# PV of four head groups per run in a fused attention and gated FFN block

## The chip, the cores and the metric

The kernel runs on one core of one Trainium2 chip. Its time is device microseconds of one execution, median of several. TensorE (PE in the profile) does the matmuls, PEld is its weight loads, VectorE is DVE, ScalarE is ACT, GpSimd is POOL, and SyncE (SP) issues most of the DMA transfers.

## The reference

One sequence of 2048 tokens of width 576 in bf16. A layer norm, then attention with 32 heads of 18 elements in a sliding window of 256 tokens, then a gated FFN of width 4608 on the same normalised input, and the two are multiplied:

```python
def _A_ref(x, wqkv, wo):
    H = 32; Dh = D // H; W = 256
    q, k, v = ...                       # (x @ wqkv) in heads
    scores = jnp.einsum("bhqd,bhkd->bhqk", q, k) * (Dh ** -0.5)
    mask = (i - j >= 0) & (i - j < W)
    p = _softmax(jnp.where(mask, scores, -1e9), axis=-1)
    o = jnp.einsum("bhqk,bhkd->bhqd", p, v)
    return o.reshape(B, S, D) @ wo

def _B_ref(x, w_gate, w_up, w_down):
    h = _sigmoid(x @ w_gate) * (x @ w_up)
    return h @ w_down

xn = _layernorm(A_x)
s = _A_ref(xn, A_wqkv, A_wo)
g = _silu(_B_ref(xn, B_w_gate, B_w_up, B_w_down))
return A_x + s * g
```

## The kernel before

The tokens are worked in four chunks of 512. For each chunk the kernel makes a graph of operations (layer norm, V, Q and K, attention of eight groups of four heads, output projection, FFN), and a list scheduler in the kernel's own Python puts the operations of all chunks into one fixed order for each engine. The engines then run their lists and wait on semaphores. FFN matmuls fill the places where attention would make TensorE wait.

Nearly all matmuls are pairs: two matmuls of 64 rows that run side by side in the two row halves of the array. All of them come from one helper, so they stand under one line (L122) in the profile:

```python
def pair(eng, outs, lhs, rhs, start, stop, swap=0):
    for i in range(2):
        t = i ^ swap
        res = eng.matmul(outs[i], lhs(ROWS[t], i), rhs(ROWS[t], i), start=start, stop=stop, tile_position=(64 * t, 0))
```

Attention of one head group computes the scores transposed, keys on the partitions, exponentiates them with ScalarE into a ring of bf16 tiles (`expr`, NEX = 12 slots), and masks the diagonal blocks with VectorE. When two head groups are ready, one PV run multiplies V by the weights. It works in tiles of 64 rows and 32 columns, eight at a time, and V carries a column of ones, so that the sum of the softmax comes out as a nineteenth row:

```python
def build_pv(self, c, pr):
    pend, self.pend = self.pend, []          # two head groups
    hp = self.pool_s.hold()                  # one PSUM unit of two banks
    def f_pv(eng):
        outs = self.halves(hp, NT)
        for n, ks in enumerate(kss):         # 12 blocks of 64 keys (8 in the first chunk)
            q0, q1 = span[ks]
            cols = slice(q0 * SW, q1 * SW)   # 64 to 320 queries
            for g, (hg, where, _) in enumerate(pend):
                for t in range(2):
                    for i in range(2):
                        res = eng.matmul(outs[i][p0:p0 + VH, cols], self.v_aug[ROWS[i], o:o + VH],
                                         self.expr[ROWS[i], se, t, cols], ...,
                                         tile_position=(64 * i, p0))
    pv = op("PE", est, f_pv, ...)            # one operation: nothing stands between its matmuls
    for i in range(2):                       # VectorE: transpose, 1/sum, multiply, transpose
        t1 = ...; hp.release(t1); rc = ...; on = ...; t2 = ...
        # then DMA of each head's rows to oT
```

The PSUM has four units: `pool_s = Pool("S", [0, 1])` for attention and `pool_f = Pool("F", [2, 3, 1])` for the FFN. The attention weights stay in SBUF for the whole run, loaded once:

```python
wq, wk, wv = (self.wqkv[:, i * D:(i + 1) * D] for i in range(3))
self.op_wqk = [self.load_nat(self.wqk[:, :, i, :], w, "dma:wqk", ...) for i, w in enumerate((wq, wk))]
self.op_wv = [self.load_nat(self.wv_sb[:, :, :], wv, "dma:wv", ...)]
self.op_wqk4 = [op("DVE", ..., copy of wqk's last 64 columns to wq4), four smaller copies]
...
self.op_wo_w = [self.load_nat(self.wo_sb[:, :, :], self.wo, "dma:wo", ...)]   # after the second head group
```

From the second chunk on, x is loaded to `xr` (two slots) and normalised into `xnr`, which a DMA transposes to `xnT`.

Of the kernel before, what the change touches and what calls it, by code (L numbers as in the profile page):

```python
# [8 lines left out]
D = 576  # L9
H = 32  # L10
DH = 18
F = 4608
P = 128
KB = 5
RD = 64
XW = D + RD
NHG = H // 4
NFT = F // P
NT = 512
# [10 lines left out]
SW = 64  # L30
# [6 lines left out]
NEX = 12  # L37
OENG = ("SP", "POOL")
PV_ORDER = (0, 5, -4, -3, -2, -1, 1, 2, 3, 4, 6, 7)
TURN_NS = 265.0  # L40
# [13 lines left out]
NXR = 2  # L54
NXN = 2
NST = 3
NQD = 2
NFIN = 2
NTH = 4
NTAIL = 112  # L60
# [13 lines left out]
NQK = 5  # L74

# [10 lines left out]
SPACE_NS = ((1500, 1500, 1400, 1500, 2000, 1200, 2000, 1100),  # L86
            (900, 1600, 1500, 1500, 1500, 2500, 1500, 1600),
            (1700, 900, 1500, 1500, 1500, 1500, 2000, 1500),
            (1500, 1500, 2500, 1100, 1600, 1500, 900, 1100))
# [4 lines left out]
def mm_ns(n):  # L94
    return max(24.7, n / 2.4 + 2.7)
# [38 lines left out]
def dve_ns(n, rate=1.0):  # L134
    return n / (0.96 * rate) + 160.0


class Hold:

    __slots__ = ("pool", "n", "units", "rel")  # L140

    def __init__(self, pool, n):
        self.pool = pool
        self.n = n
        self.units = None
        self.rel = []

    def release(self, op):
        self.rel.append(op)


class Pool:
# [27 lines left out]
    def take(self, hold, units):  # L180
        deps = []
        for u in units:
            if self.last[u] is not None:
                deps += self.last[u].rel
            self.last[u] = hold
        hold.units = units
        return deps


class Op:  # L190
# [3 lines left out]
    def __init__(self, eng, est, fn, name, deps, prio, nbytes, odeps, acq):  # L194
        self.eng = eng
        self.est = float(est)
        self.fn = fn
        self.name = name
        self.deps = []
        seen = set()  # L200
        stack = list(deps)
        while stack:
            d = stack.pop(0)
            if d is None:
                continue
            if isinstance(d, (list, tuple)):
                stack = list(d) + stack
            elif id(d) not in seen:
                seen.add(id(d))
                self.deps.append(d)  # L210
        self.prio = prio
        self.start = None
        self.end = None
        self.tok = None
        self.needs_tok = False
        self.nbytes = nbytes
        self.idx = -1
        self.succs = []
        self.cidx = -1
        self.odeps = [d for d in odeps if d is not None]  # L220
        self.acq = acq
        self.lane = None
        self.slack = 0.0
        self.filler = None
        self.space = 0.0
        for d in self.odeps:
            assert d.eng == eng

# [21 lines left out]
class Builder:  # L250
# [38 lines left out]
    def alloc_memory(self):  # L289
# [30 lines left out]
        self.ot1, _ = seq("ot1", [P, 1, NT], f32)  # L320
        self.o2, _ = seq("o2", [P, 1, NT])
        self.o2T, _ = seq("o2T", [P, 2, NT])
        self.oT, _ = seq("oT", [P, KB, NT])
        self.s_attn, _ = seq("s_attn", [P, BPC, D])
        self.wqk, _ = seq("wqk", [P, KB - 1, 2, D])
        self.wqkr, _ = seq("wqkr", [P, D])
        self.wq4, _ = seq("wq4", [P, KB, 2, RD])
        self.wv_sb, _ = seq("wv_sb", [P, KB - 1, D])
        self.wvr, _ = seq("wvr", [P, D // 2])
        self.wo_sb, _ = seq("wo_sb", [P, KB - 1, D])  # L330
        self.wor, _ = seq("wor", [P, D // 2])
        self.qd, _ = seq("qd", [P, NQD, 2, NT])
        self.xr, _ = seq("xr", [P, NXR, D])
# [23 lines left out]
    def build_graph(self):  # L357
        self.r_xr = Ring(NXR, "xr")
# [4 lines left out]
        self.r_kx = Ring(NKX, "kx")  # L363
        self.r_ex = Ring(NEX, "expr")
        self.r_ot1 = Ring(1, "ot1")
        self.r_o2 = Ring(1, "o2")
        self.r_o2T = Ring(2, "o2T")
# [19 lines left out]
        self.x_dma = {}  # L387
        self.op_wgr = {}
# [22 lines left out]
    def load_x(self, c, i=0):  # L411
# [8 lines left out]
        for _ in range(2):  # L420
            s_, d_ = self.r_xr.produce()
            slots.append(s_)
            dd += d_
        assert slots[1] == slots[0] + 1
        o = self.dma(self.xr[:, slots[0]:slots[0] + 2, :],
# [3 lines left out]
        for j in range(2):  # L429
            self.x_dma[st + j] = (o, self.xr[:, slots[j], :])  # L430
# [9 lines left out]
    def build_consts(self):  # L440
# [16 lines left out]

        wq, wk, wv = (self.wqkv[:, i * D:(i + 1) * D] for i in range(3))
        self.op_wqk = [self.load_nat(self.wqk[:, :, i, :], w, "dma:wqk", ("wqk", i), 5) for i, w in enumerate((wq, wk))]
        self.op_wqk += self.load_rem(self.wqkr[:, :], (wq, wk), "dma:wqkr", ("wqkr",), 5)  # L460
        for o in self.op_wqk:
            o.slack = 2500.0
        self.op_wv = [self.load_nat(self.wv_sb[:, :, :], wv, "dma:wv", ("wv",), 6)]
        self.op_wv += self.load_rem(self.wvr[:, :], (wv[:, 0:288], wv[:, 288:D]), "dma:wvr", ("wvr",), 6)
        for o in self.op_wv:
            o.slack = 5000.0
        self.op_wqk4 = [op("DVE", 420, lambda e: e.tensor_copy(self.wq4[:, 1:KB, :, :], self.wqk[:, :, :, 512:D]), "init:wq4",
                           deps=self.op_wqk, prio=2)]
        for t in range(2):
            for i in range(2):  # L470
                self.op_wqk4.append(op("DVE", 130, lambda e, t=t, i=i: e.tensor_copy(
                    self.wq4[ROWS[t], 0, i, :], self.wqkr[ROWS[1 - i], 512:D]), f"init:wq4:{t}{i}", deps=self.op_wqk, prio=2))
# [36 lines left out]
    def build_ln(self, c):  # L509
# [3 lines left out]
        for i in range(BPC):  # L513
# [24 lines left out]
            sn, dn = self.r_xn.produce()  # L538
# [17 lines left out]
            if c:  # L556
                self.r_xr.release(i % 2, ap)
# [56 lines left out]

    def build_qk(self, c, gi):
        op = self.op
        xs = par = c % 2
# [4 lines left out]
        gc = slice(gi * P, (gi + 1) * P)  # L622

        def lhs(r, t, k):
            if gi == 4:
                return self.wq4[r, k, :, :].rearrange("p i c -> p (i c)")
            return self.wqk[r, k - 1, t, gc] if k else self.wqkr[r, gc]
# [4 lines left out]
        pj = self.two("qk", f"{c}:{gi}", n, h, lhs, rhs, [self.op_xnT[c], self.op_wqk if gi < 4 else self.op_wqk4, dq], n)  # L632
# [44 lines left out]
    def build_v(self, c):  # L677
        op = self.op
        xs = c % 2
        for i in range(BPC):  # L680
# [5 lines left out]
            vp = self.row_proj("v", st, h, lambda r, k, cols=cols: self.xnT[r, xs, k, cols], self.wv_sb, self.wvr,  # L686
                               [self.op_xnT[c][i], self.op_wv, war])
# [16 lines left out]
    def build_attn(self, c, hg):  # L704
# [21 lines left out]
        for vi, (specs, groups) in enumerate(zip(bins, masks)):  # L726
# [27 lines left out]
            for g0, ng, m0, m1 in groups:  # L754
# [10 lines left out]
                mk = op("DVE", dve_ns(2 * ng * (m1 - m0) * SW, 2.0), f_mk, f"mk:{c}:{hg}:{vi}:{g0}", deps=[ex, self.op_mask], prio=1)  # L765
# [6 lines left out]
        if hg % 2:  # L772
            self.build_pv(c, hg // 2)
        if (c, hg) == (0, 1):
            pv = self.op_pv[(c, hg)]
            self.op_wo_w = [self.load_nat(self.wo_sb[:, :, :], self.wo, "dma:wo", ("wo",), 8, [pv])]
            self.op_wo_w += self.load_rem(self.wor[:, :], (self.wo[:, 0:288], self.wo[:, 288:D]), "dma:wor", ("wor",), 8, [pv])

    def build_pv(self, c, pr):
        op = self.op  # L780
        pend, self.pend = self.pend, []
        hp = self.pool_s.hold()
# [5 lines left out]
        def f_pv(eng):  # L788
            res = None
            outs = self.halves(hp, NT)  # L790
            for n, ks in enumerate(kss):
                q0, q1 = span[ks]
                cols = slice(q0 * SW, q1 * SW)
                for g, (hg, where, _) in enumerate(pend):
# [10 lines left out]
        est = TURN_NS + sum(mm_ns((b - a) * SW) for a, b in span.values())  # L805
# [5 lines left out]
        for i in range(2):  # L811
# [6 lines left out]
            def f_t1(e, i=i, p1=p1):  # L818
                return e.transpose(self.ot1[:, p1, :], self.halves(hp, NT)[i])  # L819
            t1 = op("DVE", dve_ns(NT), f_t1, f"ot:{c}:{pr}:{i}", deps=[pv, d1], prio=1)  # L820
            hp.release(t1)
            rc = op("DVE", 255, lambda e, o1=o1: e.reciprocal(o1[:, :, DH], o1[:, :, DH]), f"rc:{c}:{pr}:{i}", deps=[t1], prio=1)
            on = op("DVE", dve_ns(NT // 32 * DH), lambda e, o1=o1, o2=o2: e.tensor_tensor(
                o2[:, :, 0:DH], o1[:, :, 0:DH], o1[:, :, DH:VH].broadcast_to([P, NT // 32, DH]), ALU.mult),
                f"on:{c}:{pr}:{i}", deps=[rc, d2, self.op_o2z], prio=1)
            self.r_ot1.release(p1, on)
            t2 = op("DVE", dve_ns(NT), lambda e, p2=p2, p3=p3: e.transpose(self.o2T[:, p3, :], self.o2[:, p2, :]),  # L827
                    f"ot2:{c}:{pr}:{i}", deps=[on, d3], prio=1)
# [8 lines left out]
        if pr == 0:  # L837
            self.op_o[c].append(op("DVE", dve_ns(NT, 4.0), lambda e: e.tensor_copy(self.oT[ROWS[1], 0, :], self.oT[ROWS[0], 0, :]), f"odup:{c}",
                                   deps=[self.op_o[c], self.wo_last], prio=1))
# [15 lines left out]
    def build_wo(self, c):  # L855
        op = self.op
        last = []
        for i in range(BPC):
# [7 lines left out]
            wo = self.row_proj("wo", qb, h2, lambda r, k, cols=cols: self.oT[r, k, cols], self.wo_sb, self.wor,  # L866
                               [self.op_o[c], self.op_wo_w, war])
# [315 lines left out]

    def emit(self):
# [20 lines left out]

        outs = [i for lane, i in self.lane_ids.items() if lane[0] == "out"]
# [4 lines left out]
        def run_engine(e, eng):  # L1211
            known = {}
            for o in self.prog[e]:
# [4 lines left out]
                waits = {}  # L1218
                for d in o.deps:
                    k, v = d.tok  # L1220
                    if waits.get(k, -1) < v:
                        waits[k] = v
                for k, v in waits.items():
                    if known.get(k, -1) >= v:
                        continue
                    known[k] = v
                    eng.wait_ge(semof(k), v)  # L1227
# [52 lines left out]
```

The softmax here doesn't subtract the row's maximum and nothing guards it: scores larger than these inputs give would overflow.

## Time and profile before

| | |
|---|---|
| time, median of 3 | 559.3 us (558.81 to 559.37) |
| span of the profiled execution | 557.7 us |
| busy: PE, PEld, DVE, ACT, POOL | 552.4, 339.1, 333.6, 274.3, 210.3 us |
| granted TensorE clock | 1.00 throughout |
| moved by DMA | 67.83 MB, mean 122 GB/s |

The page gives each engine's busy time, the span in 40 slices, the DMA queues, the chain of work that ended last, and groups of instructions by line. L122 is the helper of the paired matmuls, L801 the matmul of PV, L819 the first transpose after PV, L764 the mask, L949 the multiplication that ends an FFN tile. A matmul's record is longer than its share of the array, since matmuls are pipelined: a 512-column pair shows 0.376 us, but the next pair starts 0.216 us after it. So costs on TensorE are read from the starts.

### The profile page before, as it was taken

The page shows a single profiled execution, that of the slowest core. Times are in us where ns is not written, and L with a number is a line of the kernel's source. Part 1 is how long each engine was busy: PE and PEld are TensorE (multiplying, and loading weights), DVE is VectorE, ACT ScalarE, POOL GpSimd, SP SyncE. Part 2 cuts the span into 40 slices and gives each one's busy share as a digit, 9 for nine tenths or more (in the row PEclk, how much of TensorE's full clock was granted, in tenths as well). Part 3 has the DMA queues.
Part 4 walks back from the last instruction along what each step waited for, and adds up shares of the span by engine and source line. Part 5 has one row for each costly group of instructions (what it writes and reads, how often), then busy time and mean ns, then how long its engine had stood idle before and what let it go on. Part 6 is the DMA issues. An engine that isn't in the chain of part 4 may idle for free.

```text
span 557.7 us, 19262 instructions
## 1 busy us (share of the span) xinstructions
PE 552.4 (99%) x8342; PEld 339.1 (61%) x8342; DVE 333.6 (60%) x797; ACT 274.3 (49%) x383; POOL 210.3 (38%) x360
## 2 busy tenths in 40 slices
PE   8999999999999999999999999999999999999997
PEld 7454444677755545457886555645588754444787
DVE  5477788787568667674558757357567623333133
ACT  4245654443656655645656464565756433223011
POOL 5564456566245454440667434034382200000000
PEclk9999999999999999999999999999999999999999
DMA  7988997831125535534121264234511035552010
GB/s 217 323 234 190 223 264 211 213 58 45 53 73 155 159 108 145 142 108 96 29 63 44 72 192 123 82 117 140 171 31 38 24 115 148 169 151 68 2 45 24
DMA packets 113468, 67.83 MB, mean 122 GB/s; under 512 B 18620, under 2 KB 111516, under 8 KB 113384
## 3 DMA queue, kind: packets, MB, share of 16 engines
q1 hardware_dynamic: 105960, 60.68, 39.7%
q0 software_dynamic: 7424, 5.92, 4.0%
q8 instruction: 66, 1.08, 0.8%
q14 instruction: 18, 0.15, 0.1%
HBM read 55.15 MB, written 2.36 MB: 103 GB/s over the span
## 4 chain that ended last, share of the span: by engine, by line
PE 98%; DVE 1%; DMA 0%; issue 0%; DVEq 0%
PE ps L122 95%; PE ps L801 3%; DMA x<-in_A_x_dram 0%; DVE small L525 0%; DVE small L527 0%; DVE xnr L541 0%; PE ps L599 0%; DVE s_attn L1062 0%; DVE thf L1067 0%; DVE xnr L545 0%; DVE small L529 0%; DVE small L531 0%; DVE xf L1072 0%; DVEq L1227 0%
## 5 line engine op out<-in xcount | busy, mean ns | idle before, releaser
L122 PE MATMUL ps<-xnT,wgs 64*128 64x512 bf16 (+1 forms) x2400 | 282.6, 368 | 0.2
L751 ACT ACTIVATE expr<-ps 128x1024 bf16<-128x1024 f32 (+4 forms) x160 | 154.9, 969 | 77.8 <-PE ps L122 77.2
L122 PEld LDWEIGHTS ps<-xnT,wgs 64*128 64x128 bf16 x2400 | 113.9, 94 | 115.0 <-DVE hT L949 1.6
L122 PE MATMUL ps<-wd_sb,hT 64*128 64x288 bf16 (+2 forms) x2448 | 156.7, 276 | 0.0
L949 DVE SCALAR_TENSOR_TENSOR hT<-tring,ps 128x512 bf16<-128x512 bf16 x144 | 98.3, 683 | 94.7 <-ACT tring L946 93.6
L946 ACT ACTIVATE tring<-ps 128x512 bf16<-128x512 f32 x144 | 86.1, 598 | 129.6 <-PE ps L122 127.5
L122 PEld LDWEIGHTS ps<-wd_sb,hT 64*128 64x128 bf16 x2448 | 112.5, 94 | 28.5
L279 POOL DMA_DIRECT2D qk<-qd x160 | 82.2, 521 | 119.9 <-PE ps L122 109.6
L764 DVE TENSOR_TENSOR expr<-expr,mask 128x128 bf16<-128x128 bf16 (+2 forms) x240 | 63.6, 299 | 62.3 <-ACT expr L751 61.7
L715 POOL TENSOR_SCALAR kx<-kprev,small 128x256 bf16<-128x256 bf16 x64 | 61.3, 967 | 28.2 <-PE ps L122 27.4
L122 PE MATMUL ps<-qk,kx 64*128 64x320 bf16 (+1 forms) x704 | 59.4, 254 | 0.0
L279 POOL DMA_DIRECT2D oT<-o2T x72 | 36.4, 513 | 58.7 <-DVE o2T L827 49.8
L122 PE MATMUL ps<-xnT,wgr 64*128 64x512 bf16 (+1 forms) x300 | 56.0, 367 | 0.0
L122 PEld LDWEIGHTS ps<-qk,kx 64*128 64x128 bf16 x704 | 31.2, 94 | 21.5 <-ACT expr L751 0.6
L122 PE MATMUL ps<-xnT,wqk 64*128 64x512 bf16 x256 | 32.6, 376 | 0.0
L1052 ACT ACTIVATE thf<-ps 128x576 bf16<-128x576 f32 (+3 forms) x22 | 11.4, 519 | 39.7 <-PE ps L122 39.4
L819 DVE STREAM_TRANSPOSE ot<-ps 128x512 f32<-128x512 f32 x32 | 22.4, 700 | 11.6 <-PE ps L801 11.5
L715 DVE TENSOR_SCALAR kx<-qk,small 128x512 bf16<-128x512 bf16 x64 | 22.4, 378 | 4.7 <-PE ps L122 4.1
L122 PEld LDWEIGHTS ps<-xnT,wgr 64*128 64x128 bf16 x300 | 14.9, 94 | 16.5
L827 DVE STREAM_TRANSPOSE o2T<-o 128x512 bf16<-128x512 bf16 x32 | 22.7, 711 | 1.0
L637 DVE CAST qd<-ps 128x1024 bf16<-128x1024 f32 (+1 forms) x20 | 22.1, 1111 | 1.5 <-PE ps L122 1.5
L697 ACT ACTIVATE v_aug<-ps 64x288 bf16<-64x288 f32 x32 | 13.1, 409 | 17.3 <-PE ps L122 16.8
(71 smaller groups left out, 300.9 us busy)
## 6 DMA issues: line engine op xcount, KB each, us to landing
wgs<-in_B_w_gate_dram SPq DMA_DIRECT2D x72, 256.0 KB, 3.3
wgs<-in_B_w_up_dram SPq DMA_DIRECT2D x72, 256.0 KB, 3.9
wd_sb<-in_B_w_down_dram SPq DMA_DIRECT2D x9, 576.0 KB, 6.3
qk<-qd POOLq DMA_DIRECT2D x100, 36.0 KB, 2.6
wgr<-in_B_w_gate_dram SPq DMA_DIRECT2D x36, 64.0 KB, 2.3
wgr<-in_B_w_up_dram SPq DMA_DIRECT2D x36, 64.0 KB, 2.7
xf<-in_A_x_dram SPq DMA_DIRECT2D x16, 144.0 KB, 2.6
out_dram<-xf SPq DMA_DIRECT2D x15, 144.0 KB, 1.8
```

Of the source, the lines that this page charges most:

```text
L122: res = eng.matmul(outs[i], lhs(ROWS[t], i), rhs(ROWS[t], i), start=start, stop=stop, tile_position=(64 * t, 0))
L279: o = self.op(eng, DMA_ISSUE_NS[eng], lambda e: e.dma_start(dst, src), name, deps, prio, nbytes=nbytes)
L637: return eng.tensor_copy(dst, self.both(h, n))
L697: return eng.activation(dst, src, ACTF.Copy)
L715: return e.tensor_scalar(self.kx[:, sx, pos:pos + n_ // SW, t, :], src.rearrange("p (s k) -> p s k", k=SW), self.half[:, t:t + 1], None, A ...
L751: return eng.activation(self.expr[:, se, :, lo * SW:NT], self.both(h, NT)[:, :, lo * SW:NT], ACTF.Exp, scale=SM_SCALE)
L764: return eng.tensor_tensor(e_, e_, m_, ALU.mult)
L801: res = eng.matmul(outs[i][p0:p0 + VH, cols], self.v_aug[ROWS[i], o:o + VH], self.expr[ROWS[i], se, t, cols], start=n == 0, stop=n == len( ...
L819: return e.transpose(self.ot1[:, p1, :], self.halves(hp, NT)[i])
L827: t2 = op("DVE", dve_ns(NT), lambda e, p2=p2, p3=p3: e.transpose(self.o2T[:, p3, :], self.o2[:, p2, :]), f"ot2:{c}:{pr}:{i}", deps=[on, d3 ...
L946: th = op("ACT", act_ns(NT), lambda e: e.activation(self.tring[:, st, :], bank(h, 0), ACTF.Tanh, scale=0.5), f"th:{c}:{ft}", deps=[pg, dt_ ...
L949: mu = op("DVE", dve_ns(NT), lambda e: e.scalar_tensor_tensor(self.hT[:, ft, :], self.tring[:, st, :], 1.0, bank(h, 1), ALU.add, ALU.mult) ...
```

## The change

PV waits for four head groups in place of two (PVG = 2 pairs), and one operation does both pairs one after the other, into two PSUM units that are given back one by one. There are eight PV runs in place of sixteen. That is meant to halve the changes between the tile shapes of PV and of everything else. Four groups need 20 slots of `expr` in place of 12. The SBUF for these comes from the attention weights: wq and wk are loaded anew in each chunk, 128 columns at a time, into a ring of two; wv and wo share one buffer and are loaded anew in each chunk, each when the other's last matmul is done; `wq4` and its copies fall away, since the last 64 columns are loaded straight into place; `xr` falls away, x being loaded into `xnr` and normalised in place; `qd` has one slot. Idle instructions (`nop`) on TensorE, spread over the FFN operations ahead of a run, are to place the run's first instruction at 80 to 124 of a block of 256 instructions. The wanted spacing of the score operations (SPACE_NS, a table for the scheduler) is set anew.

```diff
-NEX = 12
+NEX = 20
+NWQ = 2
+PVG = 2
-NXR = 2
-NQD = 2
+NQD = 1
+EVAC = (1, 0)
+HALF = 256
+PHASE = 73
+PV_PHASE = (80, 124)
+WAITS_FREE = 2
@@ SPACE_NS: all 32 values anew (cut)
@@ class Hold
+    def split(self):
+        self.parts = [Hold(self.pool, 1) for _ in range(self.n)]
@@ load_x
-        o = self.dma(self.xr[:, slots[0]:slots[0] + 2, :],
+        o = self.dma(self.xnr[:, slots[0]:slots[0] + 2, RD:XW],
@@ weights
-        self.op_wqk = [...]; self.op_wv = [...]; self.op_wqk4 = [...]; self.op_wo_w = [...]
+    def load_proj(self, c, w, name):
+        _, d = self.r_wvo.produce()
+        o = [self.load_nat(self.wvo[:, :, :], w, f"dma:{name}:{c}", ("wvo",), 6, d)]
+        o += self.load_rem(self.wvor[:, :], (w[:, 0:288], w[:, 288:D]), ...)
+    def load_qk(self, c, gi):
+        sw, d = self.r_wq.produce()
+        n = P if gi < 4 else RD
+        cols = [self.wqkv[:, i * D + gi * P:i * D + gi * P + n] for i in range(2)]
+        for i, w in enumerate(cols):
+            o.append(self.load_nat(dst, w, f"dma:wqk:{c}:{gi}", ("wqk", sw, i), 5, d))
@@ build_attn
-        if hg % 2:
-            self.build_pv(c, hg // 2)
+        if hg % (2 * PVG) == 2 * PVG - 1:
+            self.build_pv(c, hg // 2 - PVG + 1)
@@ build_pv
-        hp = self.pool_s.hold()
+        hp = self.pool_s.hold(PVG)
+        hps = hp.split()
-            outs = self.halves(hp, NT)
-            for n, ks in enumerate(kss):
+            for u, n, ks in [(u, n, ks) for u in range(PVG) for n, ks in enumerate(kss)]:
+                outs = self.halves(hps[u], NT)
-                for g, (hg, where, _) in enumerate(pend):
+                for g, (hg, where, _) in enumerate(pend[2 * u:2 * u + 2]):
-        for i in range(2):
+        for pr, hp, i in [(pr + u, hps[u], i) for u in EVAC for i in range(2)]:
@@ placing
+    def pad_pe(self):
+        ...
+            phase = (sizes[i][0] + added + PHASE) % HALF
+            mid, lo = PV_PHASE[0], PV_PHASE[1] - PV_PHASE[0]
+            need = 0 if (phase - mid) % HALF <= lo else (mid - phase) % HALF
+            hosts = [p for p in prog[first:i] if p.name.startswith("f")]
+            ...                                  # need spread over the hosts
@@ emit
+                for _ in range(pads.get(o, 0)):
+                    eng.nop()
```

## The prediction

> **What bounds the kernel now.** I read the page first (busy time, then the chain that ended last), then the waits of TensorE, then the timeline around single PV runs. The page says who is busy:
>
> ```profile
> PE 552.4 (99%) x8342; PEld 339.1 (61%) x8342; DVE 333.6 (60%) x797; ACT 274.3 (49%) x383; POOL 210.3 (38%) x360
> PEclk9999999999999999999999999999999999999999
> PE 98%; DVE 1%; DMA 0%; issue 0%; DVEq 0%
> PE ps L122 95%; PE ps L801 3%; DMA x<-in_A_x_dram 0%; DVE small L525 0%; DVE small L527 0%; DVE xnr L541 0%; PE ps L599 0%; DVE s_attn L1062 0%; DVE thf L1067 0%; DVE xnr L545 0%; DVE small L529 0%; DVE small L531 0%; DVE xf L1072 0%; DVEq L1227 0%
> ```
>
> TensorE is busy for 99% at full clock and is 98% of the chain. No other engine is above 60%, so only what shortens or lengthens the TensorE stream counts; work taken from or given to VectorE, ScalarE or the DMA queues counts only if it makes TensorE wait. Whether it waits now, the waits of its weight loads show (engine, line, what it waited for, us in total, times, longest):
>
> ```profile
> PEld ps L801 <- issue: 3.3, 10, 0.4
> PEld ps L122 <- DVE hT L949: 1.9, 6, 0.4
> PEld ps L801 <- DVE expr L764: 1.5, 4, 0.4
> ```
>
> These are idle times of the load path, most of them covered by matmuls still streaming; the longest is 0.4 us. Taking the starts of the matmuls alone, all extra gaps between the end of the warm-up (12 us) and the end add up to 1.1 us without the PV runs. So there is nearly nothing to win outside the PV runs. Around two of these runs the timeline of TensorE (start us, us, what) is:
>
> ```profile
> 62.79 0.81 PE L122 MATMUL ps<-xnT,wgs 64*128 64x512 bf16 x6
> 63.44 0.38 PE L122 MATMUL ps<-xnT,wgr 64*128 64x512 bf16 x2
> 63.74 1.01 PE L801 MATMUL ps<-expr,v_aug 64*19 64x320 bf16 x64
> 64.69 0.39 PE L122 MATMUL ps<-qk,kx 64*128 64x320 bf16 x4
> ...
> 162.93 0.81 PE L122 MATMUL ps<-xnT,wgs 64*128 64x512 bf16 x6
> 163.58 0.38 PE L122 MATMUL ps<-xnT,wgr 64*128 64x512 bf16 x2
> 163.89 1.34 PE L801 MATMUL ps<-expr,v_aug 64*19 64x320 bf16 x96
> 165.16 0.40 PE L122 MATMUL ps<-qk,kx 64*128 64x64 bf16 x6
> ```
>
> From 162.93 to 163.58 stand three pairs of 512 columns, 0.216 us a pair. The next start should come at 163.58 + 0.216 = 163.80; the PV run starts at 163.89, 0.09 us late. Its last matmuls start 1.154 us after its first and have 64 columns (0.027 us), yet the next matmul starts 0.122 us after them: another 0.095 us late. So a run costs 0.093 us to enter and 0.095 us to leave, in all sixteen runs, within 1 ns or two. The run itself takes 1.18 us with 96 matmuls (0.85 us with 64 in the first chunk), and that part is not touched.
>
> [...] PV works in 64x32 tiles and all else in 64x128; the 0.093 and 0.095 us are what the trace shows of it. [...] The trace agrees with the block size:
>
> ```profile
> q8 instruction: 66, 1.08, 0.8%
> wv_sb<-in_A_wqkv_dram SPq DMA_DIRECT2D x1, 576.0 KB, 7.5
> wo_sb<-in_A_wo_dram SPq DMA_DIRECT2D x1, 576.0 KB, 8.2
> wd_sb<-in_B_w_down_dram SPq DMA_DIRECT2D x9, 576.0 KB, 6.3
> ```
>
> 66 packets of 16 KB, one for each 256 of some 16,900 TensorE instructions (8,342 weight loads, as many matmuls, 220 waits). 0.8% of 16 engines' 557.7 us is 71 us, 1.08 us a packet. (The other three lines are loads, with KB and us to landing; they are used below.)
>
> **The change, part by part.**
>
> *Half as many PV runs.* Sixteen runs become eight; matmuls, shapes and their number (8,342) stay. Saved: 8 x (0.093 + 0.095) = 1.50 us, all on the path. A run gets 128 matmuls in the first chunk and 192 in the others, and should take 2 x 0.85 = 1.7 and 2 x 1.18 = 2.36 us, since the second half repeats the first half's shapes.
>
> *Instruction fetch.* This is the cost. A run of 192 matmuls is 384 instructions in 2.36 us, 6.15 ns each, so a block of 256 is used up in 1.57 us; in the FFN stream (four instructions in 216 ns) it lasts 13.8 us. In the trace before, the fetch packets outside PV runs mostly begin when the executing instruction is at 155 to 200 of its 256; [...] I place the moment of asking at about 160. From there a packet begins after 1.3 us in the median (up to 4.9) and takes 1.1: about 2.4 us until a block is there. A run of 192 instructions never meets two boundaries 1.57 us apart; one of 384 can. The idle instructions are to prevent it. But in the built program TensorE has 8,342 matmuls and 256 waits and no idle instruction: a nop with no wait and no count is gone after the build. So I reckon with the runs where the order puts them: their first instructions are at 94 and 188 (first chunk), 174, 191, 170, 69, 160 and 190 of 256. Those at 188 to 191 begin some 30 instructions after the asking, 1.6 us, and have 1.4 us more before the next boundary: 3 us against 2.4, mostly enough. Those at 174, 170 and 160 have 0.75 + 1.49, 0.54 + 1.51 and 1.57 us, that is 0.2 to 0.8 us too little each[...]. The run at 69 meets its second boundary only 40 instructions before its end[...]. I put 0.3 us on each of three runs and 0.1 on a fourth: 1.0 us.
>
> *Weights reloaded per chunk.* wq, wk, wv and wo are 2.65 MB; four loads in place of one bring 8 MB more on top of 67.8. The queues are busy for 44% on the mean and no TensorE wait names them, so the amount is hidden. What may show is one buffer for wv and wo: wv of the next chunk is asked for when the last wo matmul of this one is done. Adding up the durations above along the new order, the first V matmul comes 9.3, 9.9 and 6.8 us after that wo matmul. The same 576 KB landed in 6.3 us (wd_sb) to 8.2 us (wo_sb) before. Two gaps hold, the third may cost up to 1 us: I put 0.4.
>
> *LN in place, 20 expr slots, one qd slot, no wq4 copies.* These save VectorE five copies and change when buffers come free, not TensorE work. Two PSUM units per PV run instead of one keep the scores out until the transposes (L819, 0.70 us each) have read them; the new order puts FFN matmuls there, which use other units. I give this and the new spacing of scores -0.6 to +0.5 us; the 1.1 us of gaps now are all that it could win. As the order was spaced anew for this change, I take -0.6.
>
> Sum: 559.3 - 1.5 + 1.0 + 0.4 - 0.6 = 558.6 us.
>
> **Rivals.** (1) The placement doesn't matter: 256 instructions ahead are always enough, [...] as no gap of the trace before contradicts. Then the fetch costs nothing and the time is 557.5 to 557.8. Against it: the packets' late starts, up to 4.9 us after the asking. (2) The fetch becomes the bound of each long run: the sequencer has to wait at each boundary in six runs with no queued work left, some 0.8 us each, 5 us in all: 562 us. For it: 1.57 us is shorter than any fetch in the trace. Against it: only one of the two boundaries usually lies in the fast part. (3) A transfer takes the place of the wait: wv lands late, or the sync queue holds back FFN weights behind a reload that waits for a buffer; 1 to 3 us, at most 561. Against it: FFN weights have four slots, some 17 us of TensorE work ahead.
>
> **Range and chances.** All terms are of the size of 1 us, the limits are 557.1 (all saved and half of the gaps gone) and 561.0 (fetch waits in most long runs, or a late wv with some of them). More of the risk lies above than below. 2% would be 11 us: the saving cannot reach it, and a loss of that size would need a stall of 1.4 us in each run beside everything saved. Chances: faster by over 2% 0.01, within 2% 0.97, slower 0.02.
>
> **What would show it.** Right: eight PV pieces in the chain, about 1.7 and 2.36 us long, with 0.09 us lost before and after each; TensorE busy by 1 to 2 us less; no row with a wait of TensorE for wqk or wvo. Fetch waits show as PV pieces of 2.5 to 3.2 us, or as a gap just behind one, and only in those that start at 174, 170 and 160. If the long runs that start at 188 to 191 are stretched as well, rival 2 holds. A gap ahead of the first V matmul of a chunk is rival 3. The prediction is wrong if the PV runs are clean and the time has still risen, for then the new order makes TensorE wait at a place that I did not look at.

## The result

The changed kernel takes 574.75 us (573.34 to 574.90) where the kernel before takes 559.06: 1.0275 times as long, 95% interval 1.0257 to 1.0292. The prediction was 558.6 us, at most 561.0. It was wrong, by some 16 us and in the direction.

### The profile page after: what moved, and what is told of

It reads as the page before. It is cut to its first block, busy times and chain, and to the rows that moved or that the text cites. A ratio compares the mean times of both kernels' runs of the same rounds, so it can differ in the third digit from the quotient of the medians.

```text
span 572.1 us, 19381 instructions
## 1 busy us (share of the span) xinstructions
PE 556.0 (97%) x8342; PEld 349.3 (61%) x8342; DVE 331.8 (58%) x792; ACT 273.6 (48%) x383; POOL 208.8 (36%) x360
## 2 busy tenths in 40 slices
DMA packets 141341, 75.87 MB, mean 133 GB/s; under 512 B 43804, under 2 KB 139388, under 8 KB 141256
## 3 DMA queue, kind: packets, MB, share of 16 engines
HBM read 63.18 MB, written 2.36 MB: 115 GB/s over the span
## 4 chain that ended last, share of the span: by engine, by line
PE 96%; issue 2%; DVE 1%; DMA 0%; DVEq 0%
PE ps L133 93%; PE ps L838 3%; DMA x<-in_A_x_dram 0%; DVE small L538 0%; DVE small L540 0%; DVE xnr L554 0%; PE ps L610 0%; DVE s_attn L1101 0%; DVE thf L1106 0%; DVE xnr L558 0%; DVE small L542 0%; DVE small L544 0%; DVE xf L1111 0%; DVEq L1297 0%
## 5 line engine op out<-in xcount | busy, mean ns | idle before, releaser
L133 PE MATMUL ps<-xnT,wgs 64*128 64x512 bf16 (+1 forms) x2400 | 288.7, 371 | 0.3
L133 PEld LDWEIGHTS ps<-xnT,wgs 64*128 64x128 bf16 x2400 | 118.0, 94 | 112.7 <-issue 4.3
L133 PE MATMUL ps<-wd_sb,hT 64*128 64x288 bf16 (+2 forms) x2448 | 155.1, 276 | 0.9 <-issue 0.9
L133 PEld LDWEIGHTS ps<-wd_sb,hT 64*128 64x128 bf16 x2448 | 114.2, 94 | 28.5 <-issue 1.1
L133 PE MATMUL ps<-qk,kx 64*128 64x320 bf16 (+1 forms) x704 | 59.9, 254 | 0.0
L133 PE MATMUL ps<-xnT,wgr 64*128 64x512 bf16 (+1 forms) x300 | 56.8, 369 | 0.0
L133 PEld LDWEIGHTS ps<-qk,kx 64*128 64x128 bf16 x704 | 33.1, 94 | 24.2 <-ACT expr L791 1.1
L133 PE MATMUL ps<-xnT,wqk 64*128 64x512 bf16 (+1 forms) x320 | 37.8, 355 | 0.1
L838 PE MATMUL ps<-expr,v_aug 64*19 64x320 bf16 (+4 forms) x1408 | 19.7, 254 | 9.7 <-issue 9.7
L759 POOL COPY kprev<-qk 128x256 bf16<-128x256 bf16 x32 | 12.6, 400 | 38.3 <-DVE kx L755 37.0
L838 PEld LDWEIGHTS ps<-expr,v_aug 64*19 64x19 bf16 x1408 | 17.2, 86 | 13.9 <-issue 12.1
L133 PEld LDWEIGHTS ps<-xnT,wgr 64*128 64x128 bf16 x300 | 15.6, 95 | 16.3 <-issue 0.5
```

The lines of the kernel that those rows point to most:

```text
L759: self.op_kp[hg] = op("POOL", 420, lambda e: e.tensor_copy(self.kprev[:, hg, :], self.qk[:, qs, 1, NT // 2:NT]), f"kp:{c}:{hg}", deps=[kxo ...
```

## The profile after

The page of the changed kernel: busy time, granted clock in 40 slices, the chain by engine and by line (L133 is now the helper of paired matmuls, L838 the matmul of PV), and the fetch of instructions (packets, MB, share).

```profile
PE 556.0 (97%) x8342; PEld 349.3 (61%) x8342; DVE 331.8 (58%) x792; ACT 273.6 (48%) x383; POOL 208.8 (36%) x360
PEclk9999999999999989999999999989999999999999
PE 96%; issue 2%; DVE 1%; DMA 0%; DVEq 0%
q8 instruction: 66, 1.08, 0.8%
```

TensorE does the same 8,342 matmuls, but 2% of the chain is now "issue": time in which it waited for nothing that the profile shows. In two slices the clock is lower. The waits of TensorE say at which matmuls (line, what it waited for, us in total, times, longest):

```profile
PE ps L838 <- issue: 9.7, 6, 2.6
PE ps L133 <- DVE small L480: 1.1, 1, 1.1
PE ps L133 <- issue: 0.9, 1, 0.9
```

Six waits, 9.7 us, inside the six long PV runs, and one of 0.9 us behind a short one. The chain in order of time (start, us, what) has all seven; four of them:

```profile
136.81 0.91 issue
...
201.54 1.72 PE ps L838 x118
203.26 2.57 issue
205.83 0.90 PE ps L838 x47
...
316.36 1.83 issue
...
370.38 2.22 issue
```

The timeline of TensorE around the second of these (start us, us, what, idle time before it):

```profile
201.47 1.79 PE L838 MATMUL ps<-expr,v_aug 64*19 64x320 bf16 x137
205.83 0.90 PE L838 MATMUL ps<-expr,v_aug 64*19 64x256 bf16 x55 [2.57 <-issue]
```

A PV run stops in its middle for 2.57 us and then goes on. Nothing that it needs has changed meanwhile: no semaphore stands in front of these matmuls. To find what stops it, I numbered TensorE's instructions in the built program (a weight load, a matmul and a wait each count one) and looked up the first instruction after each gap over 0.3 us that has no wait of its own. In the changed kernel there are seven: 4032, 5824, 7361, 9408, 10945, 12992 and 14528. Divided by 256, all leave 192 or 193. With 66 fetch packets of 16 KB for some 16,900 instructions, a packet holds about 256 of them (an estimate, 16,900 / 66). So I take it that a block of 256 ends there (as if some 64 instructions stood ahead of the program's own), and that the gaps are waits for the next block. The packet records of the fetch fit: each of the seven gaps ends 1.2 to 1.5 us after a packet of 16 KB has landed.

In what follows the *place* of a run is the number of instructions from the last such boundary to its first matmul. The changed kernel's eight runs stand at 158 and 252 (first chunk, 256 instructions each), 238, 255, 234, 133, 224 and 254 (384 each). A matmul that starts later than the matmuls before it allow counts as a gap, and as a boundary gap if it is the first of a new block. The sums by kind, over the whole program from 9 us on, leave out the 0.09 us at each entry to and each exit from a PV run. What the matmuls before allow is a model of mine: reckoned in another way, single gaps come out up to 0.15 us larger.

| | boundary gaps us | half clock us | other gaps us | span us |
|---|---|---|---|---|
| before | 0.1 | 0 | 0.7 | 557.7 |
| changed | 12.0 | about 3 | 2.2 | 572.1 |

The half clock stands behind the two longest gaps, those of 2.73 and 2.38 us by the starts of the matmuls. Windows before, in and after such a stretch (window, its length, busy us of PE, PEld, DVE, ACT, POOL, granted clock, DMA share, GB/s):

```profile
195.00:201.00 6.00, 6.00 (x68) 3.00 (x64) 3.19 (x7) 4.05 (x5) 1.07 (x2) 1.00 0.38 110
206.80:210.40 3.60, 3.60 (x18) 1.08 (x14) 2.90 (x6) 0.60 (x1) 0.00 (x0) 0.55 0.06 15
211.00:217.00 6.00, 6.00 (x72) 3.19 (x70) 4.89 (x10) 2.81 (x4) 2.05 (x4) 1.00 0.39 109
373.90:377.50 3.60, 3.53 (x20) 0.99 (x18) 3.06 (x6) 0.60 (x1) 0.00 (x0) 0.53 0.02 5
```

After the gap that ended at 205.83 a 512-column pair starts every 0.43 us in place of 0.216. The same happens after the gap that ended at 372.60. By the clock record of the trace the clock is at 0.50 from 206.66 to 210.07 and from 373.91 to 377.33, 3.41 us each. Half of that is lost where TensorE had work: together about 3 us (an estimate, half of 2 x 3.41 less what was idle).

## The experiments

My theory now was the fetch: a block must be asked for so early that a run of 384 instructions, which uses one up in 1.57 us (an estimate, 256 at 6.15 ns), overtakes it. No trace shows the moment of asking. The 4.5 us of the expectations are an estimate too: in the changed kernel the seven late blocks took 3.4 to 5.1 us from instruction 160 of 256 until they ran. The rivals: TensorE can't be supplied with 384 such instructions wherever they stand (supply); the reloads' traffic slows the fetch or the weights (traffic); the new order or spacing makes TensorE wait (order). All experiments change the changed kernel.

**e1, idle instructions that stay.** The build removes a nop without a name (none of 626 is in the changed kernel's program); one with a name stays. The 626 then place the runs at 81, 81, 81, 98, 81, 81, 82 and 112.

```diff
                 for _ in range(pads.get(o, 0)):
-                    eng.nop()
+                    eng.nop("pad")
```

> The changed kernel with its 626 idle instructions really in the program (each nop is given a name, so that the build keeps it). Theory, fetch: a block of 256 TensorE instructions has to be asked for about 4.5 us before it runs, and only the place of a run against the block boundaries makes it wait. Then the stalls at instruction 192 of 256 inside the runs go, a run of 192 matmuls displaces 2.55 us and one of 128 matmuls 1.88 us, and the time is 557.5 us (556.5 to 560, the upper end if the runs placed at 98 and 112 meet a late block just behind them). Rival, supply: the sequencer can't supply 384 instructions at 6 ns each wherever they stand; the stalls move to another place in the run, and the time stays over 570 us. Rival, traffic: the reloads slow the fetch everywhere; half of the loss stays, 564 to 570 us.

Measured: 563.01 us against 558.95, 1.0071 times (1.0056 to 1.0086). 11.7 us of the loss are gone with nothing changed but where the runs stand. Around the third run the timeline of TensorE (start us, us, what) is now whole:

```profile
201.13 0.38 PE L133 MATMUL ps<-xnT,wgr 64*128 64x512 bf16 x2
201.44 2.46 PE L838 MATMUL ps<-expr,v_aug 64*19 64x320 bf16 x192
203.83 1.04 PE L133 MATMUL ps<-xnT,wgs 64*128 64x512 bf16 x8
```

192 matmuls without a stop: from the start that was due (201.13 + 0.216) to the next FFN matmul it displaces 2.49 us. From the first to the last start five of the six long runs take 2.273 to 2.275 us; the one at 82 loses 0.17 us at a boundary. So supply falls. But the expected 557.5 is missed, by 5.5 us. The waits show where:

```profile
PE ps L133 <- issue: 2.9, 5, 1.3
```

The gaps have moved from PV (L838) to the FFN matmuls just behind it: 0.77, 0.37, 0.66 and 1.50 us, again at instruction 192 of 256. The run at 112 has the largest, since there the next boundary comes 16 instructions behind the run.

**e2, two head groups per run with all the rest of the change.**

```diff
-PVG = 2
+PVG = 1
-EVAC = (1, 0)
+EVAC = (0,)
```

> All of the change but the length of a run: PV of two head groups per run again (16 runs of 128 or 192 to 192 instructions fewer), weights still reloaded, LN still in place, idle instructions still lost in the build. Theory, fetch: a run of 192 instructions doesn't use up a block while the next is on its way; no gap over 0.3 us at a block boundary, 559 us (558 to 561). Rival, traffic: reloads delay the fetch or the weights; gaps stay, 563 us or more. Rival, order: the new spacing and the single buffers make TensorE wait at other places; 561 to 565 us with gaps that end on waits for semaphores.

Measured: 560.61 us, 1.0032 times (1.0021 to 1.0043). One boundary gap of 0.4 us in the warm-up and one of 0.15 us, and all sixteen runs displace what they did before. It moves 75.87 MB, exactly what the changed kernel moves. So the long stalls need the long run; but reloads, new order and in-place LN cost 1.7 us by themselves.

**e3 and e4, each long run at another place.** One execution each.

```diff
-            need = 0 if (phase - mid) % HALF <= lo else (mid - phase) % HALF
+            need = (PV_AT[o.name] - phase) % HALF
+PV_AT = {...}     # e3: 61, 20, 121, 181, 102, 44; e4: 101, 180, 61, 41, 22, 144
```

(with the named nop of e1)

> Kept idle instructions, and each of the six long runs placed at another point of its block: 61, 20, 121, 181, 102, 44 (in the order of time; counted from the boundary). Theory, fetch with 4.5 us from asking to use: at 61 nearly no stall (0 to 0.3 us); at 44 about 0.7 and at 20 about 2 us, at the first boundary, inside the run; at 181 about 2 us or more at the second boundary inside it; at 102 and 121 none inside the run but 1 to 2 us just behind it, where the next boundary comes 7 to 27 instructions after the end. Rival, supply: every long run stalls by about the same. In all some 566 us by the theory.

> As the run before with the places dealt out anew: 101, 180, 61, 41, 22, 144. Theory, fetch: the stall goes with the place and not with the chunk: 101 some 1 us behind the run, 180 and 144 over 2 us at the second boundary, 61 none, 41 about 0.8, 22 about 2 us. Rival, chunk: a stall goes with the chunk's own traffic, so the third and the sixth long run stall as in the run before, whatever their place. In all some 567 us by the theory.

Measured: 571.64 and 563.81 us, so neither 566 nor 567 came true. Boundary gaps in or just behind each long run, us:

| long run | 1 | 2 | 3 | 4 | 5 | 6 |
|---|---|---|---|---|---|---|
| e3, place | 61 | 20 | 121 | 181 | 102 | 44 |
| e3, gap | 0 | 0.86 | 2.54 | 2.58 | 1.59 | 1.34 |
| e4, place | 101 | 180 | 61 | 41 | 22 | 144 |
| e4, gap | 0.40 | 1.49 | 0 | 0 | 1.25 | 1.56 |

The gap goes with the place: the third run has 2.54 us at 121 and none at 61, the fourth 2.58 at 181 and none at 41, the first none at 61. At 101 to 121 it lies behind the run, at 144 to 181 inside it, as expected. The sizes are not as expected, and a fixed time from asking to use doesn't fit: 41 gave nothing where 0.8 was expected and 44 gave 1.34, and 180 and 144 gave 1.5 where over 2 was expected. In e3 (mean granted clock 0.994) the clock fell to half again after the gaps of 2.54 and 2.58 us, and in e4 (1.0), with none over 1.6, it did not.

**e5, all runs at about 60.** `PV_AT` is 60 for each run.

> Kept idle instructions, and every run placed with its first instruction at about 60 of 256 in place of 80 to 124. Theory, fetch: at 60 both boundaries are far enough from each other and from the one before (in the two runs before, 61 gave no gap within or behind the run), so the 3.4 us of boundary gaps of the first experiment go: 559.6 us (558.8 to 560.8), with the runs at 1.88 and 2.49 us. Rival, length: a long run costs some boundary gap wherever it stands; 562 us or more. Rival, idle instructions: the idle instructions themselves delay the FFN matmuls; then the time stays near 563 us without gaps at a boundary.

Measured: 561.86 us (559.88 to 562.99), 1.0050 times (1.0037 to 1.0064). The expected 559.6 is near the best of the executions, not their median. In the profiled one four of the six long runs have no boundary gap, and they are the four with gate and up matmuls (512 columns) behind them. The two that stand in the down projection have some:

```profile
252.27 1.43 PE L839 MATMUL ps<-expr,v_aug 64*19 64x320 bf16 x98
253.97 1.32 PE L839 MATMUL ps<-expr,v_aug 64*19 64x320 bf16 x94 [0.27 <-issue]
255.22 2.26 PE L134 MATMUL ps<-wd_sb,hT 64*128 64x288 bf16 x34
257.83 0.54 PE L134 MATMUL ps<-wd_sb,hT 64*128 64x288 bf16 x6 [0.35 <-issue]
```

A down-projection pair takes 0.123 us for its four instructions, a gate pair 0.216; so the 60-odd instructions ahead of and behind the run last 1.9 us there in place of 3.3 (estimates, some 15.5 pairs of each kind). I take that for the reason of the gaps on both sides. (The brackets give idle time after the modelled end of a matmul; by the starts the gaps are 0.52 and 0.51 us.) Another 0.4 us lies inside the first run of the first chunk and 0.7 us in the warm-up. The idle instructions themselves cost nothing that shows: FFN pairs with idle instructions and no wait just ahead start on the beat of the others (75 such pairs in e1, none late; 104 in e5, the worst by 0.02 us).

**e6, reload alone.** Two groups, and slots and spacing as before:

```diff
-PVG = 2;  EVAC = (1, 0);  NEX = 20;  NQD = 1
+PVG = 1;  EVAC = (0,);    NEX = 12;  NQD = 2
-SPACE_NS = (after)
+SPACE_NS = (before)
```

> PV of two head groups per run, 12 expr slots, two qd slots and the spacing of the kernel before: what is left of the change is the reload of the weights in each chunk, LN in place and no wq4 copies. Rival theories for the 1.7 us that two groups per run with all the rest cost: if it is the reload (8 MB more, late weights, slower fetch), 560.3 to 561 us here too, with gaps that end on weights or a boundary; if it is the new spacing and the single qd slot, 558.7 to 559.5 us here.

Measured: 560.36 us (559.36 to 563.05), 1.0037 times (1.0023 to 1.0051), the same as e2. So the cost of e2 is with what the two have in common (the reload, the in-place LN and the order that the scheduler makes of them), not with the spacing or the number of slots, as far as the intervals tell. Which of these it is, no run separates. Its profiled execution has only 0.5 us more gaps than before (1.15 against 0.65 at semaphores) and a span 0.4 us longer; the executions scatter over 3.7 us, and which transfers are late in the slower ones no trace here shows.

**e7, runs at about 60 and the old spacing.** e5 with the `SPACE_NS` of the kernel before.

> As the run with every run at about 60, but with the spacing of the scores of the kernel before. If the placing alone decides, the same as that within 1 us, about 559.6 us. If the spacing matters, its gaps at semaphores differ from those there and the time lies 1 to 3 us off, more likely above, since the old spacing was chosen for another order.

Measured: 566.59 us, 1.0137 times (1.0124 to 1.0150). In its trace 4.9 us of boundary gaps and 5.4 us of others, among them three of 0.9 us at FFN matmuls some 3 us behind a long run. All three wait for the multiplication that ends an FFN tile (hT), which VectorE starts only after transposes of the run before it: the chain goes from the run's end (488.61) over the first transpose (488.63) to hT (until 491.46) and the FFN matmul (491.60). So with the runs at about 60 the new spacing was worth some 5 us, and the order counts.

**e8 and e9, no reloads.** In the second to fourth chunk wq, wk, wv and wo are not loaded again; those chunks use whatever weights the buffers hold. With the named nop, the runs stand at 61 (e8), or exactly where the changed kernel has them (e9).

```diff
     def load_proj(self, c, w, name):
         _, d = self.r_wvo.produce()
+        if c:
+            return []
     def load_qk(self, c, gi):
         sw, d = self.r_wq.produce()
+        if c:
+            return sw, []
```

> Long runs placed at 61 with kept idle instructions, and the reloads of wq, wk, wv and wo in the second to fourth chunk left out (these chunks use whatever weights the buffers hold, so they compute something else). If the reload's traffic is what makes fetches late and costs the 1.5 us, the boundary gaps of the run at 60 (3.2 us) shrink to under 1 us and the time is 557.5 to 558.5 us, the saving that was predicted. If a late fetch is the length's own affair, gaps of 2 to 3 us stay and the time is 560 to 562 us.

> The same without reloads, but each run placed where the changed kernel has it by chance (158, 252, 238, 255, 234, 133, 224, 254). If the place decides, the six long runs stall again at the second boundary, about 8 to 12 us in all, and the time is 568 to 573 us. If it was the traffic, the stalls fall to under 4 us and the time to 560 to 563 us.

Measured: 566.07 us (1.0127, 1.0106 to 1.0148) and 573.71 us (1.0262, 1.0245 to 1.0279). e9's waits of TensorE, and its transfers (packets, MB):

```profile
PE ps L843 <- issue: 8.8, 6, 2.0
DMA packets 118495, 67.90 MB, mean 119 GB/s; under 512 B 24796, under 2 KB 116540, under 8 KB 118408
```

As little traffic as before (67.9 MB), the same places, and again six waits inside the six long runs: 11.7 us of boundary gaps against 12.0. So the stall is the length's and the place's, and the traffic of the reloads falls as its cause. e8 missed both of its expectations: without the loads the scheduler makes another order, and its trace has 3.9 us of boundary gaps (2.0 in the first run alone, whose fetch packet began 6.6 us after TensorE was 64 instructions short of the boundary before) and 5.3 us of others against 2.1 in e5. It therefore doesn't price the reload. In e9 the clock stayed full, after gaps of up to 2.2 us.

## Why the prediction was wrong

**Where the loss is.** By medians: the change with short runs +1.7 us (e2), making the runs long with placing +2.4 us (e1 against e2), and losing the placing +11.7 us (changed kernel against e1); together 15.8, against 15.7 measured. In the trace, the placing's part is 8.6 us more of boundary gaps and some 3 us of half clock.

**The step that failed** is "about 2.4 us until a block is there". I summed the start of the packet (1.3) and its transfer (1.1). From the landing to the first matmul of the block there are another 1.2 to 1.5 us, in all 38 gaps over 0.3 us of these runs. Instruction 160 of 256 as the moment of asking was an estimate of mine from where the packets began; until it ran, a late block of the changed kernel took 3.4 to 5.1 us from there, as said. And the boundary is at 192: counted from where TensorE is 64 instructions short of the boundary before (a point of my choice, no moment of asking), a block that came too late took 3.6 us at the least, 4.8 in the median and 9.3 at the worst in all runs. A run goes through these 320 instructions in 1.9 us (an estimate, 320 at 6.0 ns). That is a gap, not a near thing. So the fetch wait was foreseen and its cost mis-sized: 1.0 us in the sum, 12.0 measured. For a loss of 2% the prediction asked for a stall of 1.4 us in each run and gave that 0.02; the eight runs lost 1.5 us on the mean (12.0 / 8) before the half clock.

**What stays open** is why a packet starts when it does, 1.2 to 6.6 us after that same point. Traffic meanwhile doesn't order it: among the late blocks one of the quickest (1.2 us, e4) had 302 GB/s of other transfers beside it, the slowest (6.6 us, e8) 215.

**The places** were read against the wrong boundary. So I took 188 to 191 for mostly safe and the run at 69 of my counting for nearly safe (0.1 us), and put only 0.3 us on each of the others, less than their shortfall of up to 0.8. These discounts were estimates, and no trace bears them out: all six long runs stalled, for 0.8 us at the least, and the one at 69 for 2.38 us, with two matmuls of PV left.

**The saving of 1.50 us** was right in kind and too small. Entering and leaving a run, where the tile shape changes, still cost 0.093 and 0.095 us (two of the sixteen runs before take 0.017 us more to enter, against "all sixteen"), and there are half as many. A clean run displaces 2.49 us where two before took 2 x 1.37, and 1.89 in the first chunk where two took 2 x 1.035: 1.9 us in all. The 2.36 us for a run's inside was 0.06 too high. That saving is in e1 and e5; it is about as large as the 1.7 us that the rest of the change costs.

**Lost nops.** That the idle instructions are not in the built program was right, and it is the 11.7 us. I saw it and priced it at 1.0.

**Reload, order and other gaps** were put at +0.4 - 0.6. The measurement with short runs says +1.7, so this term too was mis-sized, by 1.9 us. A late wv, my third rival, doesn't show: no gap ahead of a first V matmul in the changed kernel.

**Rivals.** The second, a fetch wait in each long run, is what happened; its "0.8 us each, 5 us in all" was the 1.57 us set against that 2.4. The first, that 256 instructions ahead are always enough, falls: one crossing of a boundary cost 0.8 to 2.7 us in each long run of the changed kernel.

**What I had no term for** is the half clock: some 3 us, behind two of the seven waits.

**Is there a version that beats both?** None of these. With no boundary gap at all the long runs would bring e2's 560.6 down by some 1.9 us, to about 558.7 (an estimate; e5's 561.9 less its 3.3 us of boundary gaps gives 558.6). That is level with the 558.9 of the kernel before. e6 shows that the rest of the change is paid even without long runs. Of what was run, the kernel before stays the fastest.

## What to carry to other kernels

Before making a stretch of small instructions longer, work out how fast it uses up its instructions and set that against the time that a late block takes, counted to the first instruction that runs and not to the landing (here 1.9 us for 320 instructions of PV, an estimate, against 3.6 us at the least). If the stretch has to be placed, look in the built program whether what places it is still there, and mind the instructions behind the stretch as much as those ahead. Here the eight entries and eight exits saved were worth 1.9 us together: the rest of the change took 1.7 of it, and one late fetch of 2 us is more than all of it.

## What the hardware showed that I had not expected

- A run of matmuls stopped for 0.8 to 2.7 us with no wait in the program and no engine to blame (six long runs of six in the changed kernel); the profile calls it "issue", and numbering the instructions shows the period of 256 (all seven gaps of the changed kernel at 192 or 193 of it).
- From the landing of a late block to its first matmul passed 1.2 to 1.5 us (38 gaps), while its packet started 1.2 to 6.6 us after TensorE was 64 instructions short of the boundary before.
- TensorE's clock fell to half for 3.41 us after gaps of 2.38 to 2.73 us (four of four, in the changed kernel and e3), and not after gaps of up to 2.2 us. A wait of 2.6 us there cost over 4 (an estimate, 2.6 and half of 3.41).
- In e1 five of the six long runs of 384 instructions went through without a stop, at 6.0 ns an instruction (2.273 to 2.275 us from the first to the last start): the rate of supply was not their limit.
